# Padding v's parts of shared token chunks to full height, and moving kvp and nu later, in a linear-attention and bilinear-FFN kernel

## The chip, the core and the metric

The kernel runs as one program on one core of a Trainium2 chip. The metric is the device time of one execution in microseconds (us). A core has a matrix engine (TensorE, PE in the rows, with its weight loads as PEld), a vector engine (VectorE, DVE), a scalar engine (ScalarE, ACT), a general one (GpSimd, POOL), a sync engine that issues most transfers here (SyncE, SP), and 16 DMA engines. Each engine works through its own instructions in order and waits on semaphores for the others. PE reads SBUF and writes to PSUM, from which DVE and ACT take the results.

## What is computed

Two stages follow each other on 4608 tokens (8 batches of 576). The first is attention by random features, with 8 heads of 64 and 128 features; the second is a bilinear feed-forward block.

```python
q_p, k_p = phi(q * s), phi(k * s)        # phi(x) = exp(h - max(h)) / sqrt(m), h = x @ omega.T - |x|^2 / 2
kv  = einsum('bhsm,bhsd->bhmd', k_p, v)  # sums over the tokens of one batch
z   = sum(k_p, axis=2)
num = einsum('bhsm,bhmd->bhsd', q_p, kv)
den = einsum('bhsm,bhm->bhs', q_p, z)[..., None] + 1e-06
x   = (num / den) as (4608, 512)
out = ((x @ w1) * (x @ w2) @ w3) @ w_out
```

The weights arrive as 64-bit floats in pairs of 32-bit words. w3 @ w_out is multiplied out once, at the start.

## The kernel before

The tokens lie in 36 chunks of 128. A batch of 576 tokens is four and a half chunks, so chunks 4, 13, 22 and 31 hold 64 tokens of one batch and 64 of the next. Every 32-bit operand is held as two 16-bit parts, high and low, and each product is three passes (high with high, high with low, low with high; PASSES, L26), accumulated in PSUM.

For a chunk c of k, `k_chunk` (L301) projects its parts on omega (kpj, L264; for q it is qpj), takes the maximum of each head (nm, L274), subtracts it (ke, L287), exponentiates (L288) and makes the two parts (ek; the low part mostly on POOL, L297). q goes the same way to qe and eq, and two DMA transposes bring eq to eqT (L364).

v's parts are made per batch: `v_norm` sums squares on ACT, `v_scale` makes one scale from them with a small matmul (norm_v, L162), and `v_split` (L325) multiplies v by it into the high part (L142 on POOL for batches 1 to 7) and subtracts for the low part (L143 on DVE). They stand in the tile vhl of the chunk, [128, 2, 8, 65], whose 65th column is a constant that yields z. A tile of a shared chunk is written by two batches, each its 64 rows. There are five such tiles in rotation (VHL_BUFS).

`kv_batch(b)` (L335) multiplies ek by vhl over the batch's five chunks into the PSUM tile kvp: 8 heads x 5 chunks x 3 passes, 120 matmuls. For the shared chunk a matmul reads only the 64 rows of this batch (`r0:r1`), so that in each head 12 matmuls are 128 rows high and 3 are 64. kvp then goes to SBUF as kv, the high part by ACT (L351), the low part by DVE (L352).

`q_attend(c)` (L366) multiplies eqT by kv into the PSUM tile nu, 24 matmuls per chunk; in a shared chunk each of two owners has its own 64 columns, 48 matmuls, one owner's three passes after the other's. DVE then makes xs from nu (L386 to L399). `x_turn` makes the parts xhl and transposes them into xT. `gate` multiplies xT by w1 and w2 (ab, L609: two PSUM tiles of 48 or 24 matmuls with 256 columns here), whose product asb is split by POOL into the arena; `project_out` multiplies that by the product of w3 and w_out (o, L635, 24 matmuls).

PSUM is shared by tag. qpj, kpj, nu and kvp all take the two buffers of tag pa (`banks`, L109), so the next of them waits until an older one has been read. ab, o and the small norms share four of tag pm.

The order of the program is written by a plan of slots. `step(i)` (L732) puts the parts of q's chunk i and k's chunk i + 5 (LEAD) into slots; a step is three slots (PACE), beginning at `at0`. At each slot the main loop (L777) first issues weight work, then one unit from a queue of gates and projections (`unit`), then what the plan holds, by rank, and then one piece of v's work (`v_unit`). From step 8 on (EARLY) q_attend stood four slots after at0 with rank 7; kv_batch stood in the last slot of its step, two slots after at0. The tile framework then settles the engines' own order and the waits from this.

Of the kernel before, what the change touches and what calls it, by code (L numbers as in the profile page):

```python
# [9 lines left out]
F32 = mybir.dt.float32  # L10
F16 = mybir.dt.float16
# [8 lines left out]
P = 128  # L20
# [5 lines left out]
PASSES = ((0, 0), (0, 1), (1, 0))  # L26
# [23 lines left out]
RESERVE = 2  # L50
EAGER = 40
EARLY = 8
RAW64_BUFS = 3
O_BUFS = 3
RAW_BUFS = 2
ASB_BUFS = 2
ARENA = 21
XT_BUFS = 3
GROUP = 2
EK_BUFS = 5  # L60
VRAW_BUFS = 5
VHL_BUFS = 5

# [2 lines left out]
def tile_favor_attention_then_bilinear_ffn(  # L66
# [19 lines left out]
    nc = tc.nc  # L86
    NCH = qT.shape[0]
    H, D = v.shape[2], v.shape[3]
    HD = H * D
    NP = H // 2  # L90
    M = omT.shape[1]
# [6 lines left out]
    E = D + 1  # L98
# [3 lines left out]
    const = ctx.enter_context(tc.tile_pool(name="const", bufs=1))  # L102
    sm = ctx.enter_context(tc.tile_pool(name="sm", bufs=4))
    at = ctx.enter_context(tc.tile_pool(name="at", bufs=2))
    mo = ctx.enter_context(tc.tile_pool(name="mo", bufs=2))
# [81 lines left out]
        return p, r  # L187


    om_raw = const.tile([P, M], F32, name="om_raw")  # L190
    nc.sync.dma_start(om_raw[0:D], omT)
    nc.sync.dma_start(om_raw[D:P], omT)
    om = const.tile([P, 2, M], F16, name="om")
# [23 lines left out]
    for i in range(4):  # L217
        t = const.tile([P, 3], F32, name=f"sums_{i}")
# [26 lines left out]
    def place(h):  # L245

        return h % 2 * NP + h // 2
# [51 lines left out]
    ek, vhl, vraw, pv, kvs = {}, {}, {}, {}, {}  # L299

    def k_chunk(c):  # L301
        e = features(c, "k")
        ek[c] = at.tile([P, 2, H, M], F16, tag="ek", name=f"ek_{c}", bufs=EK_BUFS)
        in_parts(ek[c], e, pick(EH, c), pick(EL, c))
# [19 lines left out]

    def v_split(b, n):  # L325
        c, r0, r1 = chunks_of(b)[n]
        if c not in vhl:
            vhl[c] = at.tile([P, 2, H, E], F16, tag="vhl", name=f"vhl_{c}", bufs=VHL_BUFS)
            nc.gpsimd.memset(vhl[c][:, 0, :, D : D + 1], 2.0**10)
            nc.gpsimd.memset(vhl[c][:, 1, :, D : D + 1], 0.0)  # L330
        hi, lo = (vhl[c][r0:r1, i, :, 0:D] for i in range(2))
        x = vraw[c][r0:r1]
        split(pick(VS, 5 * b + n), hi, lo, x, sv[b][r0:r1])

    def kv_batch(b):  # L335
        t = at.tile([P, 2, H, E], F16, tag="kv", name=f"kv_{b}", bufs=3)
        cs = chunks_of(b)
        ps = banks(f"kvp_{b}")[:, :, 0 : 4 * E].rearrange("p g (i e) -> p g i e", e=E)
        for h in range(H):
            mm = [(c, r0, r1, x, y) for c, r0, r1 in cs for x, y in PASSES]  # L340
            for n, (c, r0, r1, x, y) in enumerate(mm):
                nc.tensor.matmul(  # L342
                    ps[:, h // 4, h % 4],
                    ek[c][r0:r1, x, place(h)],
                    vhl[c][r0:r1, y, h],
                    start=n == 0,
                    stop=n == len(mm) - 1,
                )
        ps = ps.rearrange("p g i e -> p g (i e)")
        hi, lo = (t[:, x].rearrange("p (g i) e -> p g (i e)", g=2) for x in range(2))  # L350
        nc.scalar.mul(hi, ps, 2.0**-19)  # L351
        nc.vector.scalar_tensor_tensor(lo, ps, 2.0**-19, hi, ALU.mult, ALU.subtract)  # L352
        kvs[b] = t
# [12 lines left out]
    def q_attend(c):  # L366

        t = eqs.pop(c)
        owners = [
            (b, max(b * S - c * P, 0), min((b + 1) * S - c * P, P))  # L370
            for b in range(c * P // S, ((c + 1) * P - 1) // S + 1)
        ]
        nu = banks(f"nu_{c}")[:, :, 0 : 4 * E].rearrange("p g (i e) -> p g i e", e=E)
        for h in range(H):
            for b, r0, r1 in owners:
                for n, (x, y) in enumerate(PASSES):
                    nc.tensor.matmul(  # L377
                        nu[r0:r1, h // 4, h % 4],
                        t[:, x, place(h), r0:r1],
                        kvs[b][:, y, h],  # L380
                        start=n == 0,
                        stop=n == 2,
                    )

        gd = small("gd", H)
        nc.vector.tensor_scalar_add(  # L386
            gd.rearrange("p (g i) -> p g i", g=2), nu[:, :, :, D], 1e-6 * M * 2.0**21
        )
        gr = small("gr", H)
        nc.vector.reciprocal(gr, gd)  # L390
        xs = at.tile([P, HD], F32, tag="xs", name=f"xs_{c}", bufs=1)
        nc.vector.tensor_tensor(
            xs.rearrange("p (g i d) -> p g i d", g=2, d=D),
            nu[:, :, :, 0:D],
            gr.rearrange("p (g i) -> p g i", g=2).unsqueeze(3).broadcast_to([P, 2, 4, D]),
            ALU.mult,
        )
        mx = small("mx")
        nc.vector.tensor_reduce(mx, xs, AX.X, ALU.max, apply_absolute_value=True)  # L399
        xss[c] = xs, mx, owners  # L400
# [37 lines left out]
    arena = const.tile([P, ARENA, 512], F32, name="arena")  # L438
    raw_at = list(range(0, 4 * RAW64_BUFS, 4))
    mag_at = list(range(4 * RAW64_BUFS, 4 * RAW64_BUFS + 4, 2))  # L440
    free = list(range(4 * RAW64_BUFS + 4, ARENA))

# [186 lines left out]
    def project_out(c):  # L629
# [6 lines left out]
        for f in range(NF):  # L636
            used(hs[c, f][1])
        o = mo.tile([P, DO], F32, tag="o", name=f"o_{c}", bufs=O_BUFS)
        nc.scalar.mul(o, ps, sc)
# [46 lines left out]
    for ch in ORDER:  # L686
        n = seen.get(ch, 0)
# [17 lines left out]
    begin, slot = {}, 3  # L705
# [5 lines left out]
    def put(slot, rank, fn):  # L711
        plan.setdefault(slot, []).append((rank, len(plan[slot]) if slot in plan else 0, fn))
# [19 lines left out]
    def step(i):  # L732
        at0 = begin[i]
        kc = i + LEAD
        keys = [(n, c) for n, c in (("q", i), ("k", kc)) if 0 <= c < NCH]
        state = {}

        def norms():
            state["am"] = norm(keys, i)

        def splits():
            for name, c in keys:
                split_raw(c, name)
                if c + 2 < NCH:
                    load(srcs[name], c + 2, name)

        put(at0 - 3, 3, norms)
        put(at0 - 2, 6, lambda: scale(keys, state["am"]))
        put(at0 - 1, 8, splits)
        if i >= 0:  # L750
            put(at0, 1, lambda: q_chunk(i))
            lag = 2 if i < EARLY else 4
            put(at0 + lag, 7, lambda: q_attend(i))
            put(at0 + lag + 1, 0, lambda: ready(i))
        if kc < NCH:
            put(at0, 2, lambda: k_chunk(kc))
        if kc in B_OF_K:

            def kv():
                v_unit(len(v_work))  # L760
                kv_batch(B_OF_K[kc])

            put((begin[i + 1] if i + 1 in begin else at0 + 3) - 1, 5, kv)
        for b in range(B):
            cs = [c for c, _, _ in chunks_of(b)]
            if cs[1] == kc:
                put(at0, 9, lambda b=b: v_batch(b))
            if cs[0] == kc:
                put(at0 + 2, 10, lambda cs=cs: [v_load(c) for c in cs if c not in vraw])
# [7 lines left out]
    for t in range(max(plan) + 1):  # L777
        n = min(PER[t] if t < len(PER) else 1, len(ticks))
# [50 lines left out]
```

## Time and profile before

| what | value |
|---|---|
| three runs | 908.24 us median, 903.76 to 911.36 |
| profiled execution | 904.3 us, of which its span, first to last instruction, is 902.5 us |
| busy PE, PEld | 798.6 us (88% of the span), 597.2 us |
| busy DVE, ACT, POOL | 604.9, 408.4, 306.2 us |
| mean granted clock of TensorE | 0.935 of full speed |

Time is counted from the first instruction; 1.8 us of the profiled execution lie around its span. Busy PE is not PE at its peak: a matmul's row covers its whole passage, so matmuls that follow each other overlap, and the distance between their starts tells their price. TensorE's clock is granted at one of two levels, 1.2 or 2.4 GHz, and the profile gives it as a share of full speed for any stretch. The chain is the work that ended last, followed back from the end: at each step to what released it.

### The profile page before, as it was taken

Reading aid. Unit: us, or ns where it says so; the run is one execution under the profiler, and the core shown is the slowest. Engines: PE = TensorE matmul, PEld = TensorE weight load, DVE = VectorE, ACT = ScalarE, POOL = GpSimd, SP = SyncE. Lnnn points to the kernel's source line nnn. Section 1 sums busy time; section 2 is a strip of 40 time slices with the busy share of each in tenths; the row PEclk is TensorE's granted clock in tenths of the full one; section 3 lists DMA queues with packets and bytes.
Section 4 is the critical chain, followed back from the end, with each engine's and each line's share of the span. In section 5 each row is a group of like instructions: output and inputs, shape, how many; then the busy total and the mean of one; then the engine's idle time right before and its main releaser. Section 6 shows DMA issues by size and latency. Waiting matters only on the chain.

```text
span 902.5 us, 20479 instructions
## 1 busy us (share of the span) xinstructions
PE 798.6 (88%) x8592; PEld 597.2 (66%) x8598; DVE 604.9 (67%) x1119; ACT 408.4 (45%) x695; POOL 306.2 (34%) x319
## 2 busy tenths in 40 slices
PE   1964397678997798999989999999999999999998
PEld 1433253567685676777767777777777777777674
DVE  5879799888778359866766677567767764553210
ACT  3677765535543544554345534543554342331111
POOL 0000014233253436434543453445344542333221
PEclk9975599668998799999999999999999999999999
DMA  8535475331434323533533354334334232242100
GB/s 318 185 126 189 135 171 172 71 84 37 91 87 118 60 70 84 152 83 78 112 83 72 83 129 118 77 79 117 72 73 105 59 84 59 60 83 60 24 25 35
DMA packets 142524, 88.42 MB, mean 98 GB/s; under 512 B 116704, under 2 KB 116832, under 8 KB 142432
## 3 DMA queue, kind: packets, MB, share of 16 engines
q1 hardware_dynamic: 134944, 66.15, 31.8%
q10 hardware_dynamic: 7488, 20.97, 6.9%
q8 instruction: 67, 1.10, 0.5%
q14 instruction: 25, 0.20, 0.1%
HBM read 49.35 MB, written 9.44 MB: 65 GB/s over the span
## 4 chain that ended last, share of the span: by engine, by line
PE 58%; DVE 22%; ACT 7%; issue 5%; DMA 4%; POOL 3%; ACTq 0%; SPq 0%; DVEq 0%; POOLq 0%
PE ab L609 30%; PE o L635 14%; PE kvp L342 5%; DVE nm L274 4%; PE wp L551 3%; DVE vhl L143 3%; DVE qe L287 2%; PE nu L377 2%; DMA kraw<-kT 2%; DVE arena L480 2%; DVE asb L619 2%; PE qpj L264 1%; DVE ke L287 1%; PE kpj L264 1%; ACT ke L288 1%
## 5 line engine op out<-in xcount | busy, mean ns | idle before, releaser
L609 PE MATMUL ab<-xT,w12b 128*128 128x256 f16 (+1 forms) x3840 | 398.6, 266 | 9.2 <-DMA xT<-xhl 9.2
L609 PEld LDWEIGHTS <-w12b 128*128 128x128 f16 x3840 | 349.6, 100 | 49.7 <-DMA xT<-xhl 5.9
L635 PE MATMUL o<-Wb,arena 128*128 128x512 f16 x864 | 195.5, 380 | 2.6 <-DVE Wb L143 1.8
L635 PEld LDWEIGHTS <-arena 128*128 128x128 f16 x864 | 82.1, 98 | 96.8 <-issue 1.9
L623 POOL TENSOR_SCALAR arena<-asb 128x512 f16<-128x512 f32 x72 | 47.6, 661 | 286.4 <-DVE asb L619 252.1
L619 DVE TENSOR_TENSOR asb<-ab,asb 128x512 f32<-128x512 f32 x72 | 49.5, 687 | 107.4 <-PE ab L609 88.8
L297 POOL TENSOR_TENSOR eq<-qe,eq 128x1024 f16<-128x1024 f32 x34 | 74.3, 2187 | 136.0 <-DVE eq L129 83.2
L288 ACT ACTIVATE qe<-qe,ln_e,es 128x1024 f32<-128x1024 f32 x35 | 43.4, 1239 | 161.1 <-DVE qe L287 161.1
L624 POOL TENSOR_TENSOR arena<-asb,arena 128x512 f16<-128x512 f32 x72 | 85.5, 1187 | 6.0
L297 POOL TENSOR_TENSOR ek<-ke,ek 128x1024 f16<-128x1024 f32 x28 | 61.4, 2194 | 44.7 <-DVE ek L129 40.3
L618 ACT ACTIVATE asb<-ab 128x512 f32<-128x512 f32 x72 | 42.3, 587 | 63.0 <-PE ab L609 57.8
L342 PE MATMUL kvp<-vhl,ek 128*128 128x65 f16 x960 | 53.2, 211 | 13.3 <-POOL ek L297 6.3
L551 PE MATMUL wp<-w12b 128*128 128x512 f32 x128 | 61.0, 632 | 4.3 <-DVE w12b L481 4.3
L342 PEld LDWEIGHTS <-ek 128*128 128x128 f16 x960 | 43.5, 107 | 24.5 <-POOL ek L297 6.7
L377 PE MATMUL nu<-kv,eqT 128*128 128x65 f16 (+1 forms) x960 | 35.7, 200 | 21.9 <-DMA eqT<-eq 14.5
L377 PEld LDWEIGHTS <-eqT 128*128 128x128 f16 (+1 forms) x960 | 33.1, 106 | 26.0 <-DMA eqT<-eq 15.8
L143 DVE SCALAR_TENSOR_TENSOR qhl<-qraw,s,qhl 128x512 f16<-128x512 f32 x36 | 46.0, 1278 | 6.3 <-ACT qhl L140 6.1
L288 ACT ACTIVATE ke<-ke,ln_e,es 128x1024 f32<-128x1024 f32 x29 | 36.0, 1240 | 30.9 <-DVE ke L287 29.5
L413 ACT ACTIVATE xhl<-xs,p2r 128x512 f16<-128x512 f32 x36 | 25.8, 718 | 51.7 <-DVE p2r L186 51.5
L264 PE MATMUL kpj<-om,khl 64*128 64x128 f16 x864 | 33.8, 227 | 16.7 <-ACT khl L140 11.5
L551 PEld LDWEIGHTS wp<-w12b 128*128 128x128 f32 x128 | 25.2, 203 | 34.0 <-issue 28.4
L274 DVE TENSOR_REDUCE nm<-kpj 128x8 f32<-128x1024 f32 x36 | 43.7, 1215 | 3.4 <-PE kpj L264 3.3
(122 smaller groups left out, 983.9 us busy)
## 6 DMA issues: line engine op xcount, KB each, us to landing
kraw<-kT SPq DMA_DIRECT2D x36, 256.0 KB, 2.8
vraw<-v SPq DMA_DIRECT2D x36, 256.0 KB, 3.0
qraw<-qT SPq DMA_DIRECT2D x36, 256.0 KB, 2.7
out<-o SPq DMA_DIRECT2D x36, 256.0 KB, 2.3
arena<-w3T ACTq DMA_DIRECT2D x8, 1024.0 KB, 5.7
arena<-w ACTq DMA_DIRECT2D x8, 1024.0 KB, 5.8
arena<-wo ACTq DMA_DIRECT2D x4, 1024.0 KB, 5.4
eqT<-eq SPq DMA_TRANSPOSE x72, 3.1
```

The costliest lines, as they stand in the source:

```text
L143: nc.vector.scalar_tensor_tensor(lo, src, s, hi, ALU.mult, ALU.subtract)
L264: nc.tensor.matmul(pg[:, g, i], hl[d, x, i], om[d, y], start=first is None and n == 0, stop=n == len(PASSES) - 1,)
L274: nc.vector.tensor_reduce(nm, pj, AX.X, ALU.max, negate=True)
L288: nc.scalar.activation(e, e, AF.Exp, scale=es, bias=ln_e)
L297: (nc.vector if lo == "d" else nc.gpsimd).tensor_tensor(t[:, 1], e, t[:, 0], ALU.subtract)
L342: nc.tensor.matmul(ps[:, h // 4, h % 4], ek[c][r0:r1, x, place(h)], vhl[c][r0:r1, y, h], start=n == 0, stop=n == len(mm) - 1,)
L377: nc.tensor.matmul(nu[r0:r1, h // 4, h % 4], t[:, x, place(h), r0:r1], kvs[b][:, y, h], start=n == 0, stop=n == 2,)
L551: nc.tensor.matmul(ps, w[:, j, k * P : (k + 1) * P], guest[:, j], start=j == 0, stop=j == HALF - 1)
L609: nc.tensor.matmul(ps[:, k], w12[m][i][cc][:, a, r * P : (r + 1) * P], x[:, b, cc, off : off + T], start=j == 0, stop=j == len(mm) - 1,)
L619: nc.vector.tensor_tensor(asb, ab[1], asb, ALU.mult)
L624: nc.gpsimd.tensor_tensor(h[:, 1], asb, h[:, 0], ALU.subtract)
L635: nc.tensor.matmul(ps, hs[c, f][0][:, a], W[f][:, b], start=i == 0, stop=i == len(mm) - 1)
```

## The change

Five things are edited. (1) v's parts of a shared chunk are made once for each batch, in a tile of its own, whose other 64 rows DVE sets to zero; kvp's matmuls then always read all 128 rows. vhl tiles go from 36 to 40, in the same five buffers. (2) From step 8 on, kv_batch stands five slots after at0 in place of two. (3) From step 8 on, q_attend stands five slots after at0 with rank 0 in place of four with rank 7, and `ready`, which turns its result into gate units, a slot later too. (4) In a shared chunk, nu's passes alternate between the two owners. (5) ek has six buffers in place of five; to make room, o has two in place of three, and om_raw, used once at the start, lies in one of them.

```diff
--- before.py
+++ after.py
@@ -50,14 +50,15 @@
 RESERVE = 2
 EAGER = 40
 EARLY = 8
+KV_LAG = 5
 RAW64_BUFS = 3
-O_BUFS = 3
+O_BUFS = 2
 RAW_BUFS = 2
 ASB_BUFS = 2
 ARENA = 21
 XT_BUFS = 3
 GROUP = 2
-EK_BUFS = 5
+EK_BUFS = 6
 VRAW_BUFS = 5
 VHL_BUFS = 5
 
@@ -187,7 +188,7 @@
         return p, r
 
 
-    om_raw = const.tile([P, M], F32, name="om_raw")
+    om_raw = mo.tile([P, 512], F32, tag="o", name="om_raw", bufs=O_BUFS)[:, 0:M]
     nc.sync.dma_start(om_raw[0:D], omT)
     nc.sync.dma_start(om_raw[D:P], omT)
     om = const.tile([P, 2, M], F16, name="om")
@@ -324,11 +325,14 @@
 
     def v_split(b, n):
         c, r0, r1 = chunks_of(b)[n]
-        if c not in vhl:
-            vhl[c] = at.tile([P, 2, H, E], F16, tag="vhl", name=f"vhl_{c}", bufs=VHL_BUFS)
-            nc.gpsimd.memset(vhl[c][:, 0, :, D : D + 1], 2.0**10)
-            nc.gpsimd.memset(vhl[c][:, 1, :, D : D + 1], 0.0)
-        hi, lo = (vhl[c][r0:r1, i, :, 0:D] for i in range(2))
+        t = at.tile([P, 2, H, E], F16, tag="vhl", name=f"vhl_{b}_{c}", bufs=VHL_BUFS)
+        vhl[b, c] = t
+        if r1 - r0 < P:
+
+            nc.vector.memset(t[P - r1 : P - r0], 0.0)
+        nc.gpsimd.memset(t[r0:r1, 0, :, D : D + 1], 2.0**10)
+        nc.gpsimd.memset(t[r0:r1, 1, :, D : D + 1], 0.0)
+        hi, lo = (t[r0:r1, i, :, 0:D] for i in range(2))
         x = vraw[c][r0:r1]
         split(pick(VS, 5 * b + n), hi, lo, x, sv[b][r0:r1])
 
@@ -337,12 +341,12 @@
         cs = chunks_of(b)
         ps = banks(f"kvp_{b}")[:, :, 0 : 4 * E].rearrange("p g (i e) -> p g i e", e=E)
         for h in range(H):
-            mm = [(c, r0, r1, x, y) for c, r0, r1 in cs for x, y in PASSES]
-            for n, (c, r0, r1, x, y) in enumerate(mm):
+            mm = [(c, x, y) for c, _, _ in cs for x, y in PASSES]
+            for n, (c, x, y) in enumerate(mm):
                 nc.tensor.matmul(
                     ps[:, h // 4, h % 4],
-                    ek[c][r0:r1, x, place(h)],
-                    vhl[c][r0:r1, y, h],
+                    ek[c][:, x, place(h)],
+                    vhl[b, c][:, y, h],
                     start=n == 0,
                     stop=n == len(mm) - 1,
                 )
@@ -372,8 +376,8 @@
         ]
         nu = banks(f"nu_{c}")[:, :, 0 : 4 * E].rearrange("p g (i e) -> p g i e", e=E)
         for h in range(H):
-            for b, r0, r1 in owners:
-                for n, (x, y) in enumerate(PASSES):
+            for n, (x, y) in enumerate(PASSES):
+                for b, r0, r1 in owners:
                     nc.tensor.matmul(
                         nu[r0:r1, h // 4, h % 4],
                         t[:, x, place(h), r0:r1],
@@ -749,8 +753,8 @@
         put(at0 - 1, 8, splits)
         if i >= 0:
             put(at0, 1, lambda: q_chunk(i))
-            lag = 2 if i < EARLY else 4
-            put(at0 + lag, 7, lambda: q_attend(i))
+            lag = 2 if i < EARLY else 5
+            put(at0 + lag, 7 if i < EARLY else 0, lambda: q_attend(i))
             put(at0 + lag + 1, 0, lambda: ready(i))
         if kc < NCH:
             put(at0, 2, lambda: k_chunk(kc))
@@ -760,7 +764,8 @@
                 v_unit(len(v_work))
                 kv_batch(B_OF_K[kc])
 
-            put((begin[i + 1] if i + 1 in begin else at0 + 3) - 1, 5, kv)
+
+            put(at0 + (2 if i < EARLY else KV_LAG), 5, kv)
         for b in range(B):
             cs = [c for c, _, _ in chunks_of(b)]
             if cs[1] == kc:
```

On PE the order around nu of chunk 17 changes as follows. `ek_18` and `vhl_18` are the parts of chunk 18, the first of batch 4. Before, nu followed the small norm of the next step, and a projection stood ahead of that:

```order
L635 LDWEIGHTS arena_112
L635 MATMUL o_12_6635<-Wb_110,arena_112 128x512
L162 MATMUL norm_q19_k24_6663<-sums_3_107,ones_80 128x3
L377 LDWEIGHTS eqT_17_6171
L377 MATMUL nu_17_6671<-kv_3_4775,eqT_17_6171 128x65
```

And now the end of the same nu:

```order
L381 LDWEIGHTS eqT_17_6126
L381 MATMUL nu_17_6560<-kv_3_4994,eqT_17_6126 128x65
L163 MATMUL norm_v5_6599<-vam_5_6461,ones_80 128x8
L346 LDWEIGHTS ek_18_4861
L346 MATMUL kvp_4_6636<-vhl_4_18_5876,ek_18_4861 128x65
```

kvp of batch 4 stood a whole step earlier, between two ab units, and now follows nu of chunk 17 directly, behind the norm of batch 5's v. From there on a step on PE reads qpj, kpj, ab, norm, o, nu, (kvp), ab; it was qpj, kpj, o, norm, nu, ab, (kvp), ab.

On DVE, the rows around the low part of kv of batch 4 (`kv_4`) were these; `asb_14_0` and `asb_14_1` belong to ab units, `nm` is the maximum of the next qpj:

```order
L410 TENSOR_SCALAR pt_16_6352<-p2p1_4_6348,pv_4210 128x1
L414 SCALAR_TENSOR_TENSOR xhl_16_6354<-xs_16_6283,p2r1_4_6350,xhl_16_6354 128x512
L619 TENSOR_TENSOR asb_14_0_6342<-ab_14_0_1_6317,asb_14_0_6342 128x512
L352 SCALAR_TENSOR_TENSOR kv_4_6359<-kvp_4_6360,kv_4_6359 128x520
L619 TENSOR_TENSOR asb_14_1_6551<-ab_14_1_1_6526,asb_14_1_6551 128x512
L274 TENSOR_REDUCE nm_6581<-qpj_18_6556 128x8
```

They are now these, where `vhl_5_22` to `vhl_5_26` are v's parts of batch 5:

```order
L418 SCALAR_TENSOR_TENSOR xhl_17_6831<-xs_17_6589,p2r1_4_6827,xhl_17_6831 128x512
L332 MEMSET vhl_5_22_6609 64x1040
L144 SCALAR_TENSOR_TENSOR vhl_5_22_6609<-vraw_22_5136,s1_3_6605,vhl_5_22_6609 64x8x64
L144 SCALAR_TENSOR_TENSOR vhl_5_23_6615<-vraw_23_6313,s1_3_6605,vhl_5_23_6615 128x8x64
L144 SCALAR_TENSOR_TENSOR vhl_5_24_6620<-vraw_24_6315,s1_3_6605,vhl_5_24_6620 128x8x64
L144 SCALAR_TENSOR_TENSOR vhl_5_25_6625<-vraw_25_6317,s1_3_6605,vhl_5_25_6625 128x8x64
L144 SCALAR_TENSOR_TENSOR vhl_5_26_6630<-vraw_26_6319,s1_3_6605,vhl_5_26_6630 128x8x64
L356 SCALAR_TENSOR_TENSOR kv_4_6635<-kvp_4_6636,kv_4_6635 128x520
L623 TENSOR_TENSOR asb_14_2_6819<-ab_14_2_1_6794,asb_14_2_6819 128x512
L275 TENSOR_REDUCE nm_6860<-qpj_19_6835 128x8
```

The zeroing and the five low parts of batch 5 now stand ahead of kv of batch 4, in tiles that batch 4 gives back only when its kvp is done. The same stands at kvp of batches 2 and 6; at the odd batches no part of v is near.

## Rows read from the trace of the kernel before

**Rows 1.** Busy us by engine in two stretches (PE, PEld, DVE, ACT, POOL), clock, DMA.

```profile
0.00:299.00 299.00, 214.68 (x2236) 151.01 (x2243) 245.15 (x433) 169.39 (x314) 61.07 (x76) 0.83 0.47 135
...
450.00:750.00 300.00, 291.92 (x3389) 226.87 (x3388) 205.43 (x383) 138.38 (x222) 132.54 (x133) 1.00 0.38 88
```

**Rows 2.** PE's waits from 299 us to the end: us in total, times, longest.

```profile
PE nu L377 <- DVE qe L287: 7.3, 7, 1.8
PE kvp L342 <- POOL ek L297: 6.3, 3, 5.1
PE kpj L264 <- DVE p2p L183: 1.7, 1, 1.7
```

**Rows 3.** The chain in order of time: start us, us, what.

```profile
305.52 7.57 PE kvp L342 x106
313.10 7.42 PE ab L609 x48
...
480.89 4.84 PE kvp L342 x106
485.73 5.35 PE ab L609 x48
```

**Rows 4.** A stretch of batch 2's kvp: busy as in rows 1, then granted clock.

```profile
305.60:309.00 3.40, 3.40 (x50) 2.77 (x51) 0.00 (x0) 2.31 (x8) 1.60 (x2) 0.50 0.06 22
```

**Rows 5.** PE in order of time: nu of a shared chunk, plain nu, kvp.

```profile
416.03 0.96 PE L377 MATMUL nu<-kv,eqT 128*64 128x65 f16 x48
...
497.79 0.90 PE L377 MATMUL nu<-kv,eqT 128*128 128x65 f16 x24
498.52 10.64 PE L609 MATMUL ab<-xT,w12b 128*128 128x256 f16 x96
...
559.75 5.38 PE L342 MATMUL kvp<-vhl,ek 64*128 64x65 f16 x120
564.96 5.40 PE L609 MATMUL ab<-xT,w12b 128*128 128x256 f16 x48
```

**Rows 6.** The first matmuls of that kvp, by height (64*128 and 128*128).

```profile
559.94 0.54 PE L342 MATMUL kvp<-vhl,ek 128*128 128x65 f16 x12
560.41 0.26 PE L342 MATMUL kvp<-vhl,ek 64*128 64x65 f16 x3
560.61 0.54 PE L342 MATMUL kvp<-vhl,ek 128*128 128x65 f16 x12
```

**Rows 7.** One burst of v's parts and the nu behind it, in time.

```profile
444.64 4.66 POOL L142 TENSOR_SCALAR vhl<-vraw,s 128x512 f16<-128x512 f32 x5
445.37 5.12 DVE L143 SCALAR_TENSOR_TENSOR vhl<-vraw,s,vhl 128x512 f16<-128x512 f32 x5 [1.93 <-POOL vhl L142]
...
453.63 0.90 PE L377 MATMUL nu<-kv,eqT 128*128 128x65 f16 x24 [0.97 <-DVE qe L287]
```

**Rows 8.** A kpj that waited for kv; DVE behind nu of rows 5; ab, kpj.

```profile
94.84 0.95 PE L264 MATMUL kpj<-om,khl 64*128 64x128 f16 x24 [2.29 <-DVE kv L352]
...
500.31 0.69 DVE L392 TENSOR_TENSOR xs<-nu,gr 128x512 f32<-128x512 f32 x1
...
504.86 0.75 DVE L414 SCALAR_TENSOR_TENSOR xhl<-xs,p2r,xhl 128x512 f16<-128x512 f32 x1 [0.68 <-ACT xhl L413]
...
521.99 5.40 PE L609 MATMUL ab<-xT,w12b 128*128 128x256 f16 x48
...
528.01 0.83 PE L264 MATMUL kpj<-om,khl 64*128 64x128 f16 x24
```

**Rows 9.** Groups on DVE and POOL: busy us in total, mean ns of one.

```profile
L129 DVE CAST eq<-qe 128x1024 f16<-128x1024 f32 x34 | 23.3, 686 | 9.1 <-ACT qe L288 9.0
...
L352 DVE SCALAR_TENSOR_TENSOR kv<-kvp,kv 128x520 f16<-128x520 f32 x8 | 5.6, 699 | 30.4 <-ACT kv L351 30.4
...
L329 POOL MEMSET vhl<- 128x8 f16 x36 | 3.7, 136 | 100.5 <-PE kvp L342 100.3
...
L317 DVE MEMSET vam<- 128x8 f32 x8 | 0.5, 65 | 0.0
```

## The prediction

> **What bounds the kernel now.** First the busy time by stretch. In the first 299 us DVE is busy 245 us, PE 215, and the clock averages 0.83: there the weights are prepared and DVE leads. From 450 to 750 us PE is busy 292 of 300 us at full clock and DVE 205 [rows 1]. So from about 300 us on the time is PE's work plus PE's waits, and what PE saves there reaches the end one for one, as long as no other engine is late. Next PE's own waits after 299 us: 7.3 us of nu waiting for DVE's qe in seven places, 6.3 us of kvp waiting for POOL's low part of ek in three, 5.1 us of that in one place, and 1.7 us of one kpj [rows 2]. Little else is left, so the change is judged by these waits, by PE's own work, and by what comes late after the move. Last the chain and PE's order in time, for what lies behind each wait.
>
> **nu a unit later.** nu needs a PSUM buffer that qe must have read. Before, it stood one projection behind kpj; when a burst of v's parts kept DVE busy from 445.4 to 450.5 us, nu waited 0.97 us for qe [rows 7]. Now it stands an ab and a projection behind kpj, twice the distance. An ab unit takes 5.3 us [rows 8] and the longest such wait was 1.8 us [rows 2], so all seven go: 7.3 us. What is late next is nu's own result; xs is needed for the ab of the next group, a step later as before, and nu's buffer by the next qpj, now one ab instead of two away. nu of 497.79 was done at 498.7 and its xs at 501.0 [rows 5, 8], 2.3 us later, so one ab covers it and this costs nothing.
>
> **kvp later.** Three slots are a step, with two ab units and a projection in it; one ab alone takes 5.3 us [rows 8], and the longest wait for ek was 5.1 [rows 2]. The three waits go: 6.3 us. The long one cost more. Behind it the clock stood at 0.50 [rows 4], its level of 1.2 GHz; PE had been without work for 5 us. In the chain, 106 matmuls of kvp took 7.57 us there against 4.84 at full clock, and the next ab 7.42 against 5.35 [rows 3]: 2.7 + 2.1 = 4.8 us. Waits of up to 1.8 us left the clock at 1.00 [rows 1, 2]. I count the 4.8 us as gained.
>
> **kvp at full height.** 120 matmuls of kvp take 559.75 to 564.96, 43.4 ns each; 24 of nu, also 65 columns, take 497.79 to 498.52, 30.4 ns each [rows 5]. The rows by height show where the difference lies: a head begins at 559.94 with 12 full-height matmuls, whose row is 0.54 us for twelve and so 30 ns apart, goes to three half-height ones at 560.41 and comes back at 560.61 [rows 6]. That is 0.67 us for 15 matmuls, where 15 x 30.4 ns are 0.46. The excess of 0.21 us sits at the two changes of height. nu begins a new sum every three matmuls and pays nothing of the kind, so it isn't the new accumulation. At one height the excess goes: 120 x (43.4 - 30.4) = 1.56 us per batch, 9.4 us for batches 2 to 7, all on PE. Batches 0 and 1 lie in the first part, where the same excess is worth at most 3.1 us, but DVE leads there [rows 1]: I take 1.8 (0 to 3.1).
>
> The Trainium skill's page "TensorEngine Tiling (Array Packing)", section Theoretical Speedup, speaks against padding: a contraction of 64 rows or fewer may run up to twice as fast by packing. By that the 24 half-height matmuls of a batch would be cheap, and filling them would lose an estimated 24 x 15 ns, 3 us in eight batches. The trace shows no such gain: the three half-height matmuls take 0.20 us to the next full ones, more than 30 ns each [rows 6].
>
> **The alternating owners.** 48 half-width matmuls already take less than 0.9 us for the pair of owners [rows 5], where 24 full ones take 0.73: two run side by side already. Nothing, four times over.
>
> **What is added.** Eight zeroings on DVE of 64 x 1040 elements of 16 bits, four more pairs of small POOL memsets, all small against the idle time of both engines after 300 us. The zeroing isn't in the trace; it lies between a memset of 8 columns, 0.07 us [rows 9], and a low part of v, 5.12/5 = 1.0 us [rows 7]; I take the cast to 16 bits of 1024 columns, 0.69 [rows 9]. In the DVE-led first part two or three count: 0.5 us net (0 to 2).
>
> The Trainium skill's page "VectorE: DVE Perf Modes", section Zero memsets can be issued as uint32 (trn2), gives one cycle per element, an estimated 1.08 us for 1040 elements as they stand; by it the waits below grow by 0.4 us each. No row here shows it.
>
> The new wait is at batches 2, 4 and 6. v's parts of the next batch need tiles that kvp holds until its last matmul, and on DVE they stand ahead of kv's low part; behind kv wait asb and the next nm. kpj needs the PSUM buffer that kv's low part gives back. Count from the end of kvp. PE does one ab and qpj and stands at kpj after 528.01 - 521.99 = 6.0 us [rows 8]. POOL needs up to 1.4 us for ten memsets of 0.136 [rows 9] and 4.66 for the five high parts [rows 7]; DVE first has to end xhl: after nu it took to 505.6, 6.9 us [rows 5, 8], of which 2.2 were for the parts of q and k (an estimate, three times xhl's 0.75) that now stand ahead of nu, and kvp takes 3.7, so 1 to 1.5 us are left. It then needs 0.7 for the zeroing and 5.12 or less for the five low parts, at the least one more behind POOL's last. That ends at 6.3 to 7.4; kv's low part takes 0.7 [rows 9], so kpj can start at 7.0 to 8.1. It waits 1.0 to 2.1 us: I take 1.8, three times 5.4 us (0.7 to 4 each). Such a wait of kpj for kv stands once in the trace, 2.29 us at batch 0 [rows 8]. Around batch 2, the next nu and projections stand closer than later, and one kpj waited 1.7 us there [rows 2]; behind the later DVE I take 1.4 us more (0 to 3.5, twice that wait). o's two buffers and ek's six cost nothing: each is used once a step, of over three units of 5.3 us, and is free again a step later.
>
> **The sum.** Gained 7.3 + 6.3 + 4.8 + 9.4 + 1.8 = 29.6 us; added 0.5 + 5.4 + 1.4 = 7.3. Net 22.3 us, from the profiled 904.3 to 882.0. The median of the runs shown is 3.9 us above that execution, half their spread; I add 2 and forecast 884.0 us.
>
> **The rivals.** (A) The excess isn't the change of height but the five chunks' tiles or something that stays. Then 9.4 + 1.8 us are missing: 895. For it: no kvp of one height is in the trace. Against it: both places of the excess coincide with the height [rows 6]. (B) The waits behind v's parts come at their upper end, 4 us each, and batch 2 at 3.5: 6.6 + 2.1 us more, 893. For it: the kernel's bursts already made nu late; against it, POOL and DVE overlapped almost fully [rows 7]. (C) The first 300 us: DVE's small steps change places there, and where they come late DVE, which leads, loses 6 us in place of the net gain of 1.3, six of its passes of 1.0 us: 891. (D) Slower: one mechanism, at kpj behind batches 2, 4 and 6. If POOL's parts and DVE's don't overlap, 1.4 + 4.66 + 0.7 + 5.12 + 0.7 = 12.6 us pass before kpj, a wait of 6.6 us; that is longer than the one that lowered the clock, so 4.8 us more each time. 3 x 11.4 - 5.4 = 28.8 us above the forecast, 913, against 908. It decides from waits near the 5.1 us that lowered the clock [rows 2, 4]; from 8 us each on the kernel is slower by over 1%. Against it: the overlap in rows 7.
>
> **How the numbers follow.** The forecast 0.66, A 0.11, B 0.10, C 0.08, D 0.05. A measurement of this kernel can tell about 1% from no change: 899.2 and 917.3 us. Forecast, A, B and C alone lie below 899; two of A to C together, or a low D, lie within 1%. Faster 0.85, same 0.12, slower 0.03. The range goes down to 873: the new waits at their lower ends (4.7 us less), the first part at its full 3.1 and the zeroing free (1.8 less) make 877.5, and the runs' own spread the rest. It goes up to 899, A with half of B.
>
> **What would show it.** Right: no nu waiting for qe and no kvp waiting for ek after 300 us; kvp's row near 3.8 us for 120 matmuls at full clock; clock 1.00 at 305 to 320 us; three kpj that wait 1 to 2 us for DVE's kv. Wrong: kvp still at 5.2 us (A); kpj waits of 4 us with a lower clock behind them (B, D); batch 2's part of the program beginning over 4 us later (C).

## The result, and the profile after

The changed kernel takes 913.8 us (median of 12 runs, 910.8 to 918.0) against 907.4 us before (12 runs): a ratio of 1.0075, 95% interval 1.0053 to 1.0096. It is slower by three quarters of a per cent, where 884.0 us had been forecast. The profiled execution took 915.4 us, with a span of 913.6 us against 902.5.

Busy time by stretch (columns as in [rows 1]):

```profile
450.00:750.00 300.00, 279.06 (x3181) 215.22 (x3180) 214.08 (x374) 132.67 (x217) 140.29 (x133) 0.98 0.37 85
...
450.00:475.00 25.00, 22.62 (x234) 17.07 (x233) 17.43 (x31) 14.95 (x27) 13.35 (x9) 0.93 0.39 85
```

Between 450 and 750 us PE lost 13 us of busy time against [rows 1], and the clock is no longer at 1.00 there. PE's waits from 299 us to the end (us in total, times, longest), which answer to [rows 2]:

```profile
PE kpj L265 <- DVE kv L356: 16.0, 5, 5.5
PE kpj L265 <- DVE xs L396: 6.3, 3, 3.2
PE kpj L265 <- ACT junk_k L158: 3.0, 1, 3.0
PE kpj L265 <- DVE p2p L184: 1.7, 1, 1.7
PE qpj L265 <- DVE qhl L144: 1.1, 1, 1.1
```

The waits of nu and kvp are gone, as forecast, but kpj waits nearly twice as long as both did together: for kv three times what had been forecast (5.4 us), and for xs and junk_k, which the forecast did not name. Two places show how. Time order, all engines; the first is a step without kvp, the second batch 4:

```profile
450.82 0.90 PE L381 MATMUL nu<-kv,eqT 128*128 128x65 f16 x24
...
451.55 5.41 PE L613 MATMUL ab<-xT,w12b 128*128 128x256 f16 x48
...
452.27 2.15 POOL L298 TENSOR_TENSOR ek<-ke,ek 128x1024 f16<-128x1024 f32 x1
...
452.52 2.45 DVE L144 SCALAR_TENSOR_TENSOR qhl<-qraw,s,qhl 128x512 f16<-128x512 f32 x1 [1.21 <-ACT qhl L141]
...
454.99 0.33 SPq L213 DMA_DIRECT2D qraw<-qT  x1
...
455.90 0.15 DVE L390 TENSOR_SCALAR gd<-nu 128x8 f32<-128x8 f32 x1
...
457.76 0.63 ACT L158 ACTIVATE junk_q<-qraw 128x512 bf16<-128x512 f32 x1 [4.66 <-DMA qraw<-qT]
458.39 0.67 ACT L643 ACTIVATE o<-o,osc 128x512 f32<-128x512 f32 x1
...
459.09 0.27 DVE L635 TENSOR_SCALAR osc<-pt,kap 128x1 f32<-128x1 f32 x1 [2.80 <-ACT o L643]
459.28 0.68 DVE L396 TENSOR_TENSOR xs<-nu,gr 128x512 f32<-128x512 f32 x1
...
460.11 1.37 PE L265 MATMUL kpj<-om,khl 64*128 64x128 f16 x24 [2.38 <-DVE xs L396]
...
493.05 3.79 PE L346 MATMUL kvp<-vhl,ek 128*128 128x65 f16 x120
...
500.13 0.14 DVE L324 TENSOR_SCALAR pv<-norm_v 128x1 f32<-128x1 f32 x1
500.32 0.70 POOL L143 TENSOR_SCALAR vhl<-vraw,s 64x512 f16<-64x512 f32 x1 [3.57 <-DVE pv L324]
...
501.51 1.08 DVE L418 SCALAR_TENSOR_TENSOR xhl<-xs,p2r,xhl 128x512 f16<-128x512 f32 x1 [0.68 <-ACT xhl L417]
...
502.75 0.93 DVE L332 MEMSET vhl<- 64x1040 f16 x1 [0.16 <-issue]
...
503.71 3.84 DVE L144 SCALAR_TENSOR_TENSOR vhl<-vraw,s,vhl 64x512 f16<-64x512 f32 x5
...
507.47 0.69 DVE L356 SCALAR_TENSOR_TENSOR kv<-kvp,kv 128x520 f16<-128x520 f32 x1
508.31 1.46 PE L265 MATMUL kpj<-om,khl 64*128 64x128 f16 x24 [5.46 <-DVE kv L356]
```

Three names are new here. junk_q is the sum of squares that ACT (L158) takes of a raw chunk of q as soon as SP has loaded it; osc is the scale (DVE, L635) with which ACT's o (L643) takes an output chunk out of PSUM.

In the first place nu ends at about 451.7, but DVE takes up its result only at 455.9, behind the low parts of qhl and khl. Then it stands still: the next osc needs a buffer that ACT's o still reads, o stands behind junk_q in ACT's queue, and junk_q waits 4.66 us for a chunk of q, whose load SP could issue only when qhl's low part had freed the raw buffer. xs stands behind osc, so it ends at about 460, 8.2 us after nu, where 2.3 had been assumed. In the second place the same chain makes v's scale late (pv at 500.1, over 3 us after kvp) and xhl too (to 502.6), then come the zeroing and five low parts of v, and only then kv. Behind both waits the next matmuls take longer (kpj 1.37 and 1.46 us instead of 0.83): the granted clock of six 25-us windows after 299 us is 0.93. Batches 3 and 5, where the section on the change saw no part of v near, have one zeroing of 0.93 us ahead of kv, with a late xhl before it: kpj waits 2.4 and 2.5 us there.

kvp itself came out as forecast: 3.79 us for 120 matmuls against 5.38 in [rows 5].

An account runs from the start of nu of chunk 7 (284.98 us before, 286.93 after) to PE's last matmul (898.7 and 909.8). The waits are 13 us longer (29 against 16). What the clock cost, counted as each window's length times what its clock lacks to 1.00, is 4 us more (10.5 = 6 x 25 x 0.07, against 6.75 = 25 x 0.27 in the one slow window before). The first part ended 2 us later. The spans differ by 11 us, so 8 us are left by which PE's own work must be shorter; six kvp alone give 9.5 (6 x 1.59).

### The profile page after: what moved, and what is told of

It reads as the page before. It is cut to its first block, busy times and chain, and to the rows that moved or that the text cites. A ratio compares the mean times of both kernels' runs of the same rounds, so it can differ in the third digit from the quotient of the medians.

```text
span 913.6 us, 20527 instructions
## 1 busy us (share of the span) xinstructions
PE 790.1 (86%) x8592; PEld 589.6 (65%) x8598; DVE 633.6 (69%) x1127; ACT 405.2 (44%) x695; POOL 318.6 (35%) x327
## 4 chain that ended last, share of the span: by engine, by line
PE 44%; DVE 28%; ACT 11%; DMA 8%; issue 7%; POOL 1%; SPq 0%; another core or an unknown queue 0%; DVEq 0%; ACTq 0%; POOLq 0%
PE ab L613 23%; PE o L639 12%; DVE nm L275 5%; PE wp L555 3%; DMA qraw<-qT 3%; DVE qhl L144 3%; DVE vhl L144 2%; DMA kraw<-kT 2%; DVE qe L288 2%; DVE ke L288 2%; ACT ke L289 2%; ACT ek L132 2%; DVE arena L484 2%; PE nu L381 1%; PE kvp L346 1%
## 5 line engine op out<-in xcount | busy, mean ns | idle before, releaser
L613 PE MATMUL ab<-xT,w12b 128*128 128x256 f16 (+1 forms) x3840 | 408.7, 268 | 12.5 <-DMA xT<-xhl 10.2
L627 POOL TENSOR_SCALAR arena<-asb 128x512 f16<-128x512 f32 x72 | 57.2, 795 | 281.1 <-DVE asb L623 266.6
L639 PEld LDWEIGHTS <-arena 128*128 128x128 f16 x864 | 84.5, 100 | 94.0 <-issue 1.7
L628 POOL TENSOR_TENSOR arena<-asb,arena 128x512 f16<-128x512 f32 x72 | 89.9, 1249 | 6.0
L144 DVE SCALAR_TENSOR_TENSOR qhl<-qraw,s,qhl 128x512 f16<-128x512 f32 x36 | 63.6, 1766 | 29.1 <-ACT qhl L141 28.9
L158 ACT ACTIVATE junk_q<-qraw 128x512 bf16<-128x512 f32 x36 | 22.7, 630 | 120.6 <-DMA qraw<-qT 120.5
L635 DVE TENSOR_SCALAR osc<-pt,kap 128x1 f32<-128x1 f32 x36 | 9.7, 271 | 74.8 <-ACT o L643 74.7
L265 PEld LDWEIGHTS <-khl 64*128 64x128 f16 x864 | 28.4, 102 | 48.9 <-issue 19.1
L643 ACT ACTIVATE o<-o,osc 128x512 f32<-128x512 f32 x36 | 24.3, 674 | 52.8 <-PE o L639 52.8
L418 DVE SCALAR_TENSOR_TENSOR xhl<-xs,p2r,xhl 128x512 f16<-128x512 f32 x36 | 29.4, 815 | 24.8 <-ACT xhl L417 24.8
```

Of the source, the lines that this page charges most:

```text
L144: nc.vector.scalar_tensor_tensor(lo, src, s, hi, ALU.mult, ALU.subtract)
L265: nc.tensor.matmul(pg[:, g, i], hl[d, x, i], om[d, y], start=first is None and n == 0, stop=n == len(PASSES) - 1,)
L613: nc.tensor.matmul(ps[:, k], w12[m][i][cc][:, a, r * P : (r + 1) * P], x[:, b, cc, off : off + T], start=j == 0, stop=j == len(mm) - 1,)
L627: nc.gpsimd.tensor_scalar(h[:, 0], asb, 1.0, 1.0, ALU.mult, ALU.mult)
L628: nc.gpsimd.tensor_tensor(h[:, 1], asb, h[:, 0], ALU.subtract)
L639: nc.tensor.matmul(ps, hs[c, f][0][:, a], W[f][:, b], start=i == 0, stop=i == len(mm) - 1)
```

## The experiments

Which of the three parts costs the time was asked first. In all four runs the smaller edits (o's and ek's buffers, the alternating owners) stay as in the changed kernel. Theory N blames nu's place, theory V the separate tiles of v.

**Full height alone.** nu and kvp go back:

```diff
-            lag = 2 if i < EARLY else 5
-            put(at0 + lag, 7 if i < EARLY else 0, lambda: q_attend(i))
+            lag = 2 if i < EARLY else 4
+            put(at0 + lag, 7, lambda: q_attend(i))
-            put(at0 + (2 if i < EARLY else KV_LAG), 5, kv)
+            put((begin[i + 1] if i + 1 in begin else at0 + 3) - 1, 5, kv)
```

> v's parts made per batch at full height, with nu and kvp at their places of before. Two theories. N: what the change lost comes from nu's later place (one ab of cover between nu and the next kpj, DVE late with xs and kv). V: it comes from v's separate tiles, five for all batches, behind which the next batch's parts and kv stand. Both: kvp at one height, 3.6 us for 120 matmuls from batch 2 on instead of 5.2. N: that stays, 907 - 9 = 898 us (895 to 901). V: the waits of kpj for kv are here as well, 905 us or more.

892.8 us, 0.9843 of before (0.9797 to 0.9890): the height, with those smaller edits, gains 13.5 us. Some 3 us of that are clock: from 300 to 325 us it stands at 0.86 where it was 0.73 before, behind a wait for ek just as long. Its waits are those of before, and kpj waits 0.3 us for kv:

```profile
PE nu L381 <- DVE qe L288: 7.8, 7, 2.1
PE kvp L346 <- POOL ek L298: 6.6, 3, 5.2
```

**The places alone**, with shared tiles and two heights (`v_split` and `kv_batch` of before):

> kvp and nu at the later places, v's parts as before: one tile per chunk that two batches share, kvp at two heights. N: the new waits and the half clock stay (27 + 10 us), the gain at kvp is missing: 914 + 10 = 924 us (919 to 929). V: the waits for kv go, those before of nu and kvp are gone too: 907 - 18 = 889 us (885 to 895).

912.5 us, ratio 1.0066 (1.0040 to 1.0093). Less than N gave, but far from V's 889: the places lose by themselves.

```profile
PE kpj L265 <- DVE xs L393: 8.2, 3, 3.2
PE kpj L265 <- DVE kv L353: 6.5, 3, 3.1
```

**Height and the later kvp** (of the lines above only nu's go back), and **height and the later nu** (only kvp's line goes back):

> Full height and the later kvp, with nu at its place of before. N: kpj has two projections of cover again, so the waits for xs and kv and the half clock go; nu waits for qe again, some 7 us: 907 - 9 - 11 + 1 = 888 to 894 us. V: the waits of kpj for kv stay, 16 us of them, and the time is 905 us or more.

> Full height and the later nu, with kvp at its place of before. N: the waits of kpj for xs (6 us) and some of those for kv stay, kvp waits for ek again: 908 us or more. V: kvp stands where it stood, so the v parts behind it do too; 16 us of waits for kv stay, but if only kvp's later place makes them long they go: 892 to 898 us.

896.7 us (0.9885, 0.9839 to 0.9931) and 917.9 us (1.0119, 1.0069 to 1.0169). With nu at its old place kpj waits for kv three times, 7.1 us; with nu later and kvp old the waits for xs are back:

```profile
PE kpj L265 <- DVE kv L356: 7.1, 3, 3.8
```

```profile
PE kpj L265 <- DVE xs L396: 11.0, 3, 3.8
PE kpj L265 <- DVE kv L356: 6.6, 4, 2.4
...
PE kpj L265 <- ACT junk_k L158: 3.3, 1, 3.3
```

So theory N holds: nu's later place costs 25 us with kvp at its old place (892.8 to 917.9) and 17 with kvp later (896.7 to 913.8). kvp's later place gives 4 us in the one case and costs 4 in the other, no more than the intervals leave open. And the height, worth 13.5 us at the old places, is worth nothing at the later ones (912.5 to 913.8): the waits for kv grew from 6.5 to 16.0 us. Whether they grew because PE came to them earlier, or because the separate tiles put a zeroing ahead of kv on DVE, these runs do not separate.

Next came why nu's place is dear. **osc with seven buffers** instead of four takes DVE's wait for o away:

```diff
-        sc = small("osc")
+        sc = small("osc", bufs=7)
```

> The changed kernel with seven buffers for osc instead of four. Theory O: xs is late because DVE holds it behind an osc whose buffer ACT's o still reads, and that o stands on ACT behind a junk_q that waits for its load. Then the waits of kpj for xs (6.3 us) and for junk_k (3.0) go, the long one for kv shrinks by 2.7, and some 5 us of half clock with them: 914 - 17 = 897 us (893 to 902). Rival L: nu's place itself is too late, whatever osc does (the parts of q and k stand ahead of gd, one ab follows): less than 6 us of it goes, 908 to 914.

903.2 us (0.9963, 0.9937 to 0.9989): 10.6 us come back, of 17 expected. No kpj waits for xs or junk_k any more, but the waits for kv are 19.0 us, so these are not osc's.

**kv ahead of the next batch's parts of v.** The slot of kv emitted all of v's waiting work first, for batches 0, 2, 4 and 6 the next batch's:

```diff
-                v_unit(len(v_work))
+                if i < EARLY or B_OF_K[kc] % 2:
+                    v_unit(len(v_work))
```

> The changed kernel, but at batches 0, 2, 4 and 6 after the first eight chunks the slot of kv no longer emits the next batch's v work ahead of kvp, so that on DVE kv's low part stands ahead of the next batch's low parts of v. Theory V: these parts hold kv back; the waits of kpj for kv fall from 16 us to under 5 and half the low clock goes: 914 - 11 - 5 = 898 us (894 to 903). Rival: kv is behind xs and osc rather than behind v's parts, 907 us or more.

> Both edits, osc with seven buffers and kv ahead of the next batch's v parts. If the two orders on DVE are all that the change lost by, waits after 299 us fall to about 6 us and low clock to about 2 us in place of 29 and 10: 914 - 31 = 883 us (878 to 889), what was forecast for the change. If nu's later place itself loses (L), 895 us or more.

Alone 913.7 us (1.0082, 1.0053 to 1.0111), no gain: the waits for kv fell to 10.8 us, but those for xs rose to 10.3; why they rose is open. Theory V falls as a single cause here. Both edits give 897.9 us (0.9905, 0.9873 to 0.9938), 16 us back and not the 31 expected. What is left is kv, 12.9 us in four waits, now with only the zeroing of v's tile ahead of it on DVE, and that behind xhl:

```profile
568.58 3.79 PE L346 MATMUL kvp<-vhl,ek 128*128 128x65 f16 x120
...
574.32 0.63 ACT L158 ACTIVATE junk_q<-qraw 128x512 bf16<-128x512 f32 x1 [4.62 <-DMA qraw<-qT]
...
577.80 0.71 ACT L417 ACTIVATE xhl<-xs,p2r 128x512 f16<-128x512 f32 x1
578.42 0.58 ACT L355 ACTIVATE kv<-kvp 128x520 f16<-128x520 f32 x1
578.54 0.75 DVE L418 SCALAR_TENSOR_TENSOR xhl<-xs,p2r,xhl 128x512 f16<-128x512 f32 x1 [3.22 <-ACT xhl L417]
...
580.52 0.70 DVE L356 SCALAR_TENSOR_TENSOR kv<-kvp,kv 128x520 f16<-128x520 f32 x1
581.37 0.85 PE L265 MATMUL kpj<-om,khl 64*128 64x128 f16 x24 [2.98 <-DVE kv L356]
```

kvp ended at about 572.2, but ACT's high parts of xhl and kv stand behind o and the junks, and these behind the load of qraw. So the load itself became the suspect. Over the whole second part ACT waits for it as follows, before and after:

```profile
ACT junk_q L157 <- DMA qraw<-qT: 23.8, 19, 3.7
```

```profile
ACT junk_q L158 <- DMA qraw<-qT: 106.1, 25, 5.8
```

ACT's queue through a step, as its instructions stand in the program: first before, then in the changed kernel.

```
L639 ACTIVATE o_8522<-o_8497,osc 128x512
L140 ACTIVATE qhl_8634<-qraw_8039,s_4_8529 128x512
L140 ACTIVATE khl_8639<-kraw_8044,s_4_8529 128x512
L618 ACTIVATE asb_2_8618<-ab_2_0_8568 128x512
L413 ACTIVATE xhl_8630<-xs_8562,p2r_4_8626 128x512
L157 ACTIVATE junk_q_9069,sums_107<-qraw_8637 128x512
L157 ACTIVATE junk_k_9071,sums_107<-kraw_8642 128x512
```

```
L141 ACTIVATE qhl_8300<-qraw_7588,s_4_8207 128x512
L141 ACTIVATE khl_8305<-kraw_7593,s_4_8207 128x512
L158 ACTIVATE junk_q_8738,sums_105<-qraw_8303 128x512
L643 ACTIVATE o_8240<-o_8215,osc 128x512
L158 ACTIVATE junk_k_8740,sums_105<-kraw_8308 128x512
L417 ACTIVATE xhl_8375<-xs_8296,p2r_4_8370 128x512
```

Before, o stood ahead of the parts of q and k, and an ab's asb and mostly xhl lay between these and the junks, time for most of the load. With nu, and so xhl, a unit later, junk_q moved up right behind qhl and khl, ahead of o, and both junks ahead of xhl, in almost every step. ACT's wait of junk_q for qraw goes with nu's place in the four runs above: 27.3 and 23.6 us with nu at its old place, 109.7 and 118.7 with nu later.

**Three buffers for q's raw chunks** (kv gets two, for room), on the changed kernel and on the kernel with both edits:

```diff
-        t = at.tile([P, NP, P], F32, tag=f"{name}raw", name=f"{name}raw_{c}", bufs=RAW_BUFS)
+        t = at.tile([P, NP, P], F32, tag=f"{name}raw", name=f"{name}raw_{c}", bufs=3 if name == "q" else 2)
-        t = at.tile([P, 2, H, E], F16, tag="kv", name=f"kv_{b}", bufs=3)
+        t = at.tile([P, 2, H, E], F16, tag="kv", name=f"kv_{b}", bufs=2)
```

> The changed kernel with three buffers for q's raw chunks instead of two (kv gets two instead of three, for room), so that the load of qraw no longer waits for the low part of qhl. Theory R: that load is the root of the late o on ACT, and so of the late osc and xs on DVE; ACT's wait of junk_q for qraw (120 us in all) falls under 40, the waits of kpj for xs go, as with more buffers for osc: 914 - 11 = 903 us (899 to 906). Rival: junk_k, whose load still waits for khl, holds ACT at the same time as before, with o, xhl and kv's high part behind it: 910 us or more.

> All three edits: three buffers for q's raw chunks, seven for osc, kv ahead of the next batch's v parts. 897.9 us with the last two alone, where kpj still waits 12.9 us for kv, behind xhl on DVE and, on ACT, behind junk_q's load. If that load is the root, these waits and the half clock behind them shrink to a third: 898 - 9 - 5 = 884 us (879 to 890). Rival: junk_k and the junks of v on ACT hold xhl and kv's high part as long: 895 us or more.

909.6 us (1.0037, 1.0014 to 1.0059) and 909.1 us (1.0039, 1.0008 to 1.0069). The first is 4 us less than the changed kernel, with the waits for xs down to 0.6 us, as theory R had it, but those for kv up from 16.0 to 21.1. The second is 11 us more than with the two edits alone (897.9), where 14 less had been expected; its waits for kv rose from 12.9 to 16.2 us. The rivals were right: k's load takes q's place. In the first of the two:

```profile
ACT junk_k L158 <- DMA kraw<-kT: 81.8, 20, 5.9
...
ACT junk_q L158 <- DMA qraw<-qT: 17.1, 4, 5.0
```

And in the second, at batch 5, where ACT's high parts of xhl and kv stand behind it:

```profile
577.86 0.63 ACT L158 ACTIVATE junk_k<-kraw 128x512 bf16<-128x512 f32 x1 [6.08 <-DMA kraw<-kT]
```

**Both loads early**, on the kernel with the height and the later nu, and as a control on the one with the height alone. Three raw buffers for q and for k (RAW_BUFS) need room, which kvp's old place gives (ek with five buffers). With two tiles of sums instead of four, junk_q can't run a step ahead into the same wait, as the order laid out with four has it:

```diff
-RAW_BUFS = 2
+RAW_BUFS = 3
-EK_BUFS = 6
+EK_BUFS = 5
-    for i in range(4):
+    for i in range(2):
         t = const.tile([P, 3], F32, name=f"sums_{i}")
```

> Full height and the later nu, kvp at its place of before (917.9 us so far, kpj waiting 11.0 for xs, 6.6 for kv, 3.3 for junk_k), now with three raw buffers for q and for k and two tiles of sums, by which the loads go out a step earlier and ACT's queue has junk_q and junk_k ahead of qhl, and o and xhl right behind khl. Theory R: ACT's wait for these loads, with o, xhl and kv behind it, is what makes nu's later place dear; its wait of junk_q falls from over 100 us to under 20, the waits of kpj for xs, kv and junk_k fall under 6 us together, the half clock of 10 us to 2: 918 - 15 - 8 = 895 us (889 to 899). Rival L: the place itself is too late on DVE, behind the parts of q and k: 908 us or more.

> The same edit of loads and sums on full height with nu and kvp at their places of before (892.8 us). There ACT waits 42 us for the loads too, but no kpj waits behind it: 893 us (890 to 896), no gain. If the earlier loads shorten PE's own path by something else, 888 us or less, and the gain in the run with the later nu would not be due to nu's place.

With the later nu: 881.6 us (0.9739, 0.9700 to 0.9777), 36 us less than without the edit. With nu at its old place: 885.0 us (0.9765, 0.9718 to 0.9812), 8 us less, where none were expected (there nu's waits fell from 7.8 to 5.1 us and kvp's from 6.6 to 2.8). That is the case named beforehand in which the gain is not due to nu's place, and it holds for 8 of the 36 us; 28 come with the later nu alone. In the first of these ACT has no wait of junk_q for qraw left in the list, and PE's waits of 0.4 us and over after 299 us are down to:

```profile
PE kvp L346 <- POOL ek L298: 3.0, 2, 2.7
PE kpj L265 <- DVE khl L144: 1.7, 1, 1.7
PE nu L381 <- DVE qe L288: 0.4, 1, 0.4
PE qpj L265 <- DVE qhl L144: 0.4, 1, 0.4
```

The step that answers to the first place above, in time order:

```profile
443.81 0.63 ACT L158 ACTIVATE junk_q<-qraw 128x512 bf16<-128x512 f32 x1
...
444.31 2.14 POOL L298 TENSOR_TENSOR ek<-ke,ek 128x1024 f16<-128x1024 f32 x1
...
444.81 0.90 PE L381 MATMUL nu<-kv,eqT 128*128 128x65 f16 x24
...
445.93 1.07 DVE L144 SCALAR_TENSOR_TENSOR qhl<-qraw,s,qhl 128x512 f16<-128x512 f32 x1 [2.58 <-ACT qhl L141]
...
448.79 0.67 ACT L643 ACTIVATE o<-o,osc 128x512 f32<-128x512 f32 x1
...
450.11 0.69 DVE L396 TENSOR_TENSOR xs<-nu,gr 128x512 f32<-128x512 f32 x1
...
451.56 0.83 PE L265 MATMUL kpj<-om,khl 64*128 64x128 f16 x24
```

junk_q runs ahead of the parts of q, without a wait; xs begins 4.4 us after nu's end instead of 7.6; one ab covers it, and kpj doesn't wait. Theory R holds: nu's later place is dear because of these loads and ACT's order, not by itself. The edit changes both at once, the buffers and, by the sums, the order, so which of the two counts for more is not shown. Nor was it run with kvp at its later place. This kernel beats the one before and the changed one. Between it and its control the intervals overlap: that nu's later place now gains is not shown, though nu's waits for qe fell from 5.1 to 0.4 us.

Two tries at a better place for kvp, with nu at its old place: **three slots later at batch 2 alone**, and **one slot later everywhere**:

```diff
-            put(at0 + (2 if i < EARLY else KV_LAG), 5, kv)
+            put(at0 + (5 if B_OF_K[kc] == 2 else 2), 5, kv)
```

```diff
-            put(at0 + (2 if i < EARLY else KV_LAG), 5, kv)
+            put(at0 + (2 if i < EARLY else 3), 5, kv)
```

> Full height, nu at its place of before, kvp at its place of before but for batch 2, where it stands three slots later. If that place is worth its wait for ek (5.2 us), the half clock behind it (3.5) less a wait for kv of 1.2 us as seen with all batches later: 892.8 - 7 = 886 us (883 to 889). Rival: what is won there comes back as waits of kpj or in the first part, 891 us or more.

> Full height, nu at its place of before, and kvp one slot later than before, behind the next chunk's two projections, instead of three. One ab and two projections (7 us) cover the wait for ek of 5.2 us and the two of 0.7, the half clock of 3.5 us goes, and kv's low part has two ab units until the next projection: 892.8 - 10 = 883 us (880 to 887). Rival: kvp now waits for ke's read of its PSUM buffer or nu waits behind it, several us, and the time is 891 us or more.

891.6 us (0.9820, 0.9784 to 0.9855), not to be told from 892.8 and as its rival had it (891 or more): the waits for ek fell from 6.6 to 1.4 us, those for kv rose from 0.3 to 2.9. And 907.6 us (1.0024, 1.0002 to 1.0046): there kvp waits for qe's read of the PSUM buffer.

```profile
PE kvp L346 <- DVE qe L288: 14.6, 5, 4.0
```

## Why the prediction was wrong

**kvp at one height** was right. 3.79 us against 5.38 is 1.59 us a batch, 1.56 had been worked out, and the height gains 13.5 us where 11.2 were forecast for it, some 3 of the 13.5 by the clock. The Trainium skill's page "TensorEngine Tiling (Array Packing)", section Theoretical Speedup, gives a speedup of up to 2x for a small dimension of 64 or less. No such gain shows in kvp, where three half-height matmuls stand among twelve full ones: filling them made it faster.

**The alternating owners** were put at nothing, and nothing shows: 48 matmuls of a shared chunk's nu take 0.95 us, 0.96 before. **nu's waits for qe and kvp's for ek** went, as forecast (7.3 and 6.3 us), and so did the slow clock from 300 to 325 us at batch 2.

**"so one ab covers it and this costs nothing"** failed: this is the step that decided. The 2.3 us from nu to xs were read from one place of the trace of before, with DVE's and ACT's queues as they stood then. (The place was typical: from 300 us on the median is 2.3 us there, though the longest is 6.0; in the changed kernel they are 3.6 and 9.1.) But the move laid these queues out anew: the parts of q and k came ahead of nu's result on DVE, and junk_q, with its load, ahead of o and xhl on ACT. The first of these the prediction knew: in its count behind kvp it took the parts of q and k as done before nu. They ran behind it, 2.45 and 1.09 us, so that DVE took up nu's result 4.2 us after its end. The second it did not have. xs then came 8.2 us after nu, more than one ab. The runs put 17 to 25 us on this place, and with kvp at its old place the early loads took it away.

**"It waits 1.0 to 2.1 us"**, for kpj behind v's parts, named the right mechanism and mis-sized it here: three waits were forecast at 5.4 us, five came with 16.0, at batches 2 to 6: 11.0 us at the three forecast, 5.0 at batches 3 and 5. With nu at its old place the three of the forecast stand alone with 7.1 us, close to it. At batch 4 the term that was off is DVE's rest of xhl, put at 1 to 1.5 us after kvp: it ended some 6 us after. POOL's start 3.6 us after kvp was not in the count either. Both lie behind the late xs there; but osc's buffers, which cured xs, left 19.0 us of these waits, so xs is not their whole cause, and no run with both kvp and nu later is free of them.

**The clock.** That waits of up to 1.8 us leave it at 1.00 was taken from before. The new waits were taken as equally harmless; six windows at 0.93 cost 10.5 us. Length alone did not decide: behind the wait of 1.99 us at batch 2 the clock stood at 0.76 from 333 to 340 us, while behind those of 2.52 us (588 us) and 3.04 us (646 us) it stayed at 1.00. Rival D had this as its mechanism, with kv waits of 6.6 us at three batches: the time it gave, 913 us, is that measured, but by luck. Only one of the waits came near (5.5 us), and the cause was another.

**The first part** is not resolved: nu of chunk 7 starts at 281.9 to 287.7 us over all profiled kernels, in no order by edit. A gain of 1.3 us can't be seen in that.

The sum: a net gain of 22 us was forecast, and the profile shows a loss of 11. Of these 33 us, 20 are waits (29 where 8.5 had been left or added), 8 clock (10.5 where 2 had been left), 2 PE's work (8 gained, by what the account leaves, 9.4 forecast) and 3 the first part (2 lost, 1.3 gained).

## What to carry to other kernels

When an instruction moves in a kernel whose queues are laid out by rank and readiness, read on every engine what now stands ahead of its result, not only whether the buffer it needs is far enough away: here a load that nothing on PE had waited for came to stand ahead of three results that PE needs. More buffers at the chain's last link (osc) gave back 10.6 us; both loads early, with two tiles of sums and kvp at its old place, 36. One load early alone moved the wait to the other load. And a saving on PE isn't yet time: the height gave 13.5 us where few waits followed, nothing where many did.

## What the runs showed of the hardware

Two of DVE's durations differed from what was taken. The zeroing of 64 x 1040 elements of 16 bits took 0.93 us where 0.69 had been chosen. The Trainium skill's page "VectorE: DVE Perf Modes", section Zero memsets can be issued as uint32 (trn2), came nearer, with an estimated 1.08 us; the measurement decides.

The low part of qhl, the same instruction on the same tile shape, took 2.45 us in the changed kernel and 1.07 in the one with early loads (rows above). In the first it ran beside POOL's low part of ek (to 454.42 us), in the second mostly behind it (to 446.45). The Trainium skill's page "GPSIMD Engine Reference", section Specifications, says that POOL shares its SBUF interfaces with VectorE and contends with DVE instructions that have two SBUF inputs, as this one has; these rows agree. The price is up to 1.7 us: in the kernel before, the 22 low parts of q and k from 299 us on with nothing on POOL beside them took 0.69 to 0.75 us, such as this one:

```profile
502.88 0.74 DVE L143 SCALAR_TENSOR_TENSOR khl<-kraw,s,khl 128x512 f16<-128x512 f32 x1
```

From 300 us on the low part of qhl took over 2.3 us in 17 of 27 chunks of the changed kernel, in none of the kernel before and in none with the early loads. So nu's later place also made DVE slower ahead of nu's result. No run takes this alone away; with osc's seven buffers it stands in 16 of 27 chunks, and yet no kpj waits for xs.
